# Attention with the heads' dimensions on partitions instead of tokens, in blocks of 384 tokens

## The chip, the core and the metric

The kernel runs on one core of a Trainium2 chip. TensorE (PE) multiplies matrices into PSUM, VectorE (DVE) and ScalarE (ACT) read and write PSUM and the arena in on-chip memory, and SyncE (SP) issues the DMA transfers from its queue. The metric is the device time of one execution in microseconds.

## What is computed

Linear attention over 4 batches of 576 tokens with 8 heads of 64 dimensions, a norm over each head, one dense network with 2,048 hidden units, and a mixture of 8 experts with 1,024 hidden units, whose weights come out of 8 rounds of normalizing.

```python
def _attn_ref(q, k, v, g_norm):                       # (4, 8, 576, 64)
    kv = np.einsum('bhsd,bhse->bhde', k, v)
    out = np.einsum('bhsd,bhde->bhse', q, kv)
    rms = np.sqrt(np.mean(out * out, axis=-1, keepdims=True) + 1e-06)
    return (out / rms * g_norm)

def _moe_ref(x, w_in, w_out, alpha):                  # 512 -> 2048 -> 512
    h = x @ w_in
    g = np.maximum(h, 0.0) + alpha * np.minimum(h, 0.0)
    return (g @ w_out)

def _moe2_ref(x, w_gate, w1, w2):                     # 8 experts, 512 -> 1024 -> 512
    P = normalized(np.exp(x @ w_gate - max))          # 8 rounds over rows and columns
    for e in range(E):
        out += P[:, e:e + 1] * (np.maximum(x @ w1[e], 0.0) @ w2[e])
```

The 2,304 tokens are 4 batches one behind the other, 512 features each (8 heads of 64).

## The kernel before

The large products run as 7 instead of 8 smaller ones each (a scheme of sums and differences of quarters), and each operand is split into two fp16 halves, of which three products are made. `hi_lo_mms` (line 397) issues them all: 12,240 products with 384 or 256 columns. The tokens are worked on in three pairs `p` of two blocks of 384 (`NB`); a layer `e` runs over the pairs, `Quad` units make its hidden values, `Ys` or `Outs` its results. The dense network is layers 0 and 1, the experts are layers 2 to 9. For layer 0 each pair needs the seven operands `X[m]` of x, in both halves, with features on partitions and tokens along the line.

All weights of the dense network arrive as raw words, 16 chunks for each layer, which `from_f64` turns into numbers with VectorE and ScalarE. After 8 chunks of w_in SyncE's queue holds k, v and q of the batches in an order that `FIRST` sets (line 25), then chunks of w_out. `attn_kv` (from line 435) multiplies k and v of a batch, 20 fp32 products, and writes the result into `kvbd`, 128 x 128 for two heads, with zeros between heads.

`attn_tile` makes the attention of 128 tokens, 18 times. The q tile is the stationary operand and `kvbd` streams through it (line 477), so tokens are on partitions and features along the line. ScalarE squares, VectorE sums over the 64 dimensions of each head, seven small steps on 8 columns make the inverse root with a correcting step, and VectorE multiplies by it. `attn_x` then makes the seven operands for 128 tokens of both blocks of a pair, in steps of 256 columns, into buffers of two operands, and `send` lets a DMA transpose each buffer into `X`. SyncE issues these transposes, twelve for each pair. `attn_store` copies X of pairs 0 and 1 to DRAM for layer 1. The first product that needs operand `m` waits for the transposes of it (`mx_part`).

The last two q blocks share one buffer. The first of them is loaded when the second w_in staging buffer is free (`st_free[1]`), the second when the first has been used (`load_q`).

No instruction's place is written out by hand. `Sched` is a planner: each step is a generator that yields an engine, a cost and a call, and a list scheduler with a model of each engine sets one fixed order for each engine; eight dry passes refine the due times, and the best one is issued. `T(0.87, ...)` is a TensorE step with a cost of 0.87 us. `LAGS` holds priorities. So a change to any step can move all the others. Engines then run their lists in order and wait by semaphores.

Almost every instruction of VectorE and ScalarE has line 163, where the planner issues it; on TensorE line 163 holds the small fp32 products that are issued directly.

Of the kernel before, what the change touches and what calls it, by code (L numbers as in the profile page):

```python
# [26 lines left out]
SQUARES = "000000000000000000"  # L27
# [3 lines left out]
LENT = 3  # L31
# [226 lines left out]
def fused_kernel(ctx: ExitStack, tc: tile.TileContext, qT, k, v, g_norm, w_in, w_out, alpha,  # L258
# [7 lines left out]
    nc = tc.nc  # L266
# [34 lines left out]
    def program(sc):  # L301
# [25 lines left out]
        one = const(1)  # L327
# [83 lines left out]
        x1s = [view(BR + t * 2048, F32, D) for t in range(NTILE)]  # L411
        batches = [sorted({(t * P) // S, ((t + 1) * P - 1) // S}) for t in range(NTILE)]
        kv_loaded, kv_done = [ev(2) for _ in range(4)], [ev() for _ in range(4)]
        q_loaded, q_used = [ev() for _ in range(NBLK)], [ev(TPB) for _ in range(NBLK)]
        x1_done = [ev() for _ in range(NTILE)]
# [37 lines left out]
        norm_bufs = Slots(sc, [[const(H) for _ in range(3)] for _ in range(5)])  # L453

        def by_heads(dst, x, f, **kw):
            for h in range(H):
                sl = slice(h * HD, (h + 1) * HD)
                nc.scalar.activation(dst[:, sl], x[:, sl], f, **{k_: a[:, h:h + 1] for k_, a in kw.items()})

        def attn_tile(t):  # L460

            j, o = divmod(t, TPB)
            q, x1 = qs[j], x1s[t]
            yield q_loaded[j]
            if t >= NTILE - LENT:
                yield mx_done[0]
            for b in batches[t]:
                yield kv_done[b]
            buf = yield from norm_bufs.get()
            ss, rr, tb = buf  # L470
            ps = yield from banks.get()

            def mms():
                for p in range(DC):
                    for b in batches[t]:
                        r0, r1 = max(b * S - t * P, 0), min((b + 1) * S - t * P, P)
                        nc.tensor.matmul(ps[r0:r1, p * P:(p + 1) * P], q[:, p, o * P + r0:o * P + r1],  # L477
                                         kvbd[b][:, p, :], start=True, stop=True)
            yield T(0.87 * len(batches[t]), mms)
            q_used[j].set()  # L480
            if SQUARES[t] == "1":
                yield "A", 1.93, by_heads, (x1, ps, AF.Square), dict(accum_out=ss)
            else:
                yield A(D, nc.scalar.activation, x1, ps, AF.Square)
                yield V(D, nc.vector.tensor_reduce, ss, x1.rearrange("p (h e) -> p h e", h=H), op=add, axis=AX.X)
            yield ts(H, ss, ss, 2.0 ** -20 / HD, 1e-6 * 2.0 ** -20, mult, add)
            yield A(H, nc.scalar.activation, rr, ss, AF.Sqrt)
            yield V(H, nc.vector.reciprocal, rr, rr)
            yield tt(H, tb, rr, rr, mult)
            yield tt(H, tb, tb, ss, mult)  # L490
            yield ts(H, tb, tb, -0.5, 1.5, mult, add)
            yield tt(H, rr, rr, tb, mult)
            yield [V(D, nc.vector.tensor_tensor, x1.rearrange("p (h e) -> p h e", h=H),
                     ps.rearrange("p (h e) -> p h e", h=H),
                     rr.rearrange("p (h o) -> p h o", o=1).to_broadcast([P, H, HD]), op=mult),
                   ("A", 1.93, by_heads, (x1, ps, AF.Copy), dict(scale=rr))]
            banks.put(ps)
            norm_bufs.put(buf)
            x1_done[t].set()


        MADE = (2, 0, 1, 4, 6, 5, 3)
        XPOS = [MADE.index(m_) for m_ in range(7)]
        X = view(XR, F16, 7, 2, 2 * NB).rearrange("p m a (c n) -> p m a c n", c=2)
        XF, XT = view(XR, F16, 7 * 4 * NB), view(XR, F16, 7 * 4, NB)
        half_slots = [view(TR + 18432 + i * 2048, F16, 2, D) for i in range(3)]
        lent = [view(BR + t * 2048, F16, 2, D) for t in range(NTILE - LENT, NTILE)]
        half_slots = [Slots(sc, half_slots + lent), Slots(sc, half_slots)]
        mx_split, mx_done, mx_stored = [ev(TPB) for _ in range(NP)], [ev() for _ in range(NP)], \
            [ev() for _ in range(NP)]  # L510

        def attn_x(p, o):

            even, odd = 2 * p * TPB + o, (2 * p + 1) * TPB + o
            yield x1_done[even]
            yield x1_done[odd]
            if p > 0:
                yield mx_done[0]
                yield s1_used[0][p - 1]
                yield mx_stored[p - 1]  # L520
            b11, b21, b12, b22 = [x1s[t][:, i * 256:(i + 1) * 256] for t in (even, odd) for i in range(2)]

            def send(n, buf):
                k = min(2, 7 - 2 * n)
                yield "S", 1.27, nc.sync.dma_start_transpose, (), dict(
                    out=XT[:, 8 * n:8 * n + 4 * k, o * P:(o + 1) * P], in_=buf[:, 0:k].rearrange("p k d -> p (k d)"))
                sc.dma_free = max(sc.dma_free, sc.now) + 0.45 * k
                yield sc.dma_free + 1.0
                half_slots[p > 0].put(buf)
                mx_part[p][n].set()  # L530

            bufs = []

            def put(x):
                n, k = divmod(len(bufs), 2)
# [928 lines left out]
```

## Time and profile before

| | us |
|---|---|
| median of 3 runs | 1846.12 (1844.31 to 1850.98) |
| profiled execution | 1846.93 |
| its span, first to last instruction | 1845.1 |
| TensorE busy | 1741.9 (94%), 12,808 products and as many weight loads |
| VectorE busy | 1535.5 (83%) |
| ScalarE busy | 1080.7 (59%) |
| mean granted clock of TensorE | 0.986 of 2.4 GHz |

The busy times are of the whole span. TensorE's fp32 products are recorded as two records each, so a matrix product in fp32 counts twice among the 12,808. Durations of neighbours on one engine overlap, so a mean duration is more than the distance from start to start. The page's division of the span into 40 slices shows TensorE at nine tenths or more from the sixth slice on, and at less in four of the first five, which are some 231 us.

### The profile page before, as it was taken

Reading aid. Unit: us, or ns where it says so; the run is one execution under the profiler, and the core shown is the slowest. Engines: PE = TensorE matmul, PEld = TensorE weight load, DVE = VectorE, ACT = ScalarE, POOL = GpSimd, SP = SyncE. Lnnn points to the kernel's source line nnn. Section 1 sums busy time; section 2 is a strip of 40 time slices with the busy share of each in tenths; the row PEclk is TensorE's granted clock in tenths of the full one; section 3 lists DMA queues with packets and bytes.
Section 4 is the critical chain, followed back from the end, with each engine's and each line's share of the span. In section 5 each row is a group of like instructions: output and inputs, shape, how many; then the busy total and the mean of one; then the engine's idle time right before and its main releaser. Section 6 shows DMA issues by size and latency. Waiting matters only on the chain.

```text
span 1845.1 us, 32006 instructions
## 1 busy us (share of the span) xinstructions
PE 1741.9 (94%) x12808; PEld 1251.7 (68%) x12808; DVE 1535.5 (83%) x3381; ACT 1080.7 (59%) x2290; POOL 2.5 (0%) x8
## 2 busy tenths in 40 slices
PE   4659899999999999998999999999999999999999
PEld 3435466666677766776777777677767777776777
DVE  5999696769788999699869978986998699789866
ACT  4666564535477676457646656764676556567544
POOL 0000000000000000000000000000000000000000
PEclk9789999999999999999999999999999999999999
DMA  9927411302021021112201210211122012101121
GB/s 291 256 87 189 95 62 54 121 12 86 21 106 61 12 95 47 61 47 82 76 11 47 106 61 1 81 72 61 47 83 84 1 47 106 61 1 60 59 95 35
DMA packets 70470, 137.36 MB, mean 74 GB/s; under 512 B 38960, under 2 KB 46640, under 8 KB 67632
## 3 DMA queue, kind: packets, MB, share of 16 engines
q1 hardware_dynamic: 67568, 135.28, 22.0%
q8 instruction: 100, 1.64, 0.4%
q10 hardware_dynamic: 2752, 0.03, 0.1%
q14 instruction: 50, 0.41, 0.1%
HBM read 108.55 MB, written 18.48 MB: 69 GB/s over the span
## 4 chain that ended last, share of the span: by engine, by line
PE 75%; DVE 15%; ACT 2%; DMA 2%; issue 0%; ACTq 0%; SPq 0%; DVEq 0%
PE ps L397 75%; DVE arena L163 15%; ACT arena L163 2%; DMA arena<-arena 1%; PE ps L163 0%; PE ps L683 0%; DMA arena<-in_w_in_dram 0%; ACTq L163 0%; SPq L163 0%; DVEq L163 0%
## 5 line engine op out<-in xcount | busy, mean ns | idle before, releaser
L397 PE MATMUL ps<-arena 128*128 128x256 f16 (+1 forms) x12240 | 1692.9, 301 | 72.4 <-ACT arena L163 33.9
L397 PEld LDWEIGHTS <-arena 128*128 128x128 f16 x12240 | 1200.6, 98 | 555.5 <-issue 88.3
L163 ACT ACTIVATE arena<-arena 128x384 f16<-128x384 f32 (+6 forms) x1528 | 797.1, 569 | 276.1 <-DVE arena L163 222.5
L163 DVE TENSOR_TENSOR arena<-arena 128x384 f16<-128x384 f32 (+7 forms) x1647 | 841.5, 555 | 47.5 <-ACT arena L163 43.9
L163 ACT ACTIVATE arena<-ps 128x384 f32<-128x384 f32 (+3 forms) x655 | 291.4, 451 | 410.2 <-PE ps L397 384.7
L163 DVE SCALAR_TENSOR_TENSOR arena<-ps,arena 128x384 f32<-128x384 f32 (+1 forms) x447 | 247.3, 555 | 108.9 <-PE ps L397 97.8
L163 DVE SCALAR_TENSOR_TENSOR arena<-arena 128x384 f32<-128x384 f32 (+3 forms) x526 | 283.8, 550 | 15.9 <-ACT arena L163 11.9
L163 DVE TENSOR_TENSOR arena<-ps,arena 128x256 f32<-128x256 f32 (+1 forms) x233 | 101.0, 438 | 102.5 <-ACT arena L163 73.4
L163 DVE TENSOR_REDUCE arena<-arena 128x1 f32<-128x1024 f32 (+7 forms) x148 | 112.0, 760 | 2.7 <-ACT arena L163 1.1
L163 ACT ACTIVATE arena<-ps,arena 128x384 f32<-128x384 f32 x96 | 55.1, 577 | 60.8 <-PE ps L397 57.9
L163 DVE TENSOR_SCALAR arena<-arena 128x8 f32<-128x8 f32 (+9 forms) x241 | 53.3, 235 | 5.6 <-DMA arena<-in_w_in_dram 4.8
L445 PE MATMUL ps<-arena 128*128 128x128 f32 (+1 forms) x160 | 26.2, 311 | 26.3 <-DMA arena<-in_v_dram 26.3
L445 PEld LDWEIGHTS ps<-arena 128*128 128x128 f32 (+1 forms) x160 | 22.0, 205 | 30.2 <-issue 27.1
L163 DVE TENSOR_SCALAR_CACHE_REDUCE arena<-arena 128x512 f32<-128x512 f32 x32 | 21.4, 677 | 7.5 <-ACT arena L163 7.5
L477 PE MATMUL ps<-arena 128*128 128x128 f32 (+1 forms) x160 | 18.3, 278 | 0.3 <-ACT arena L163 0.3
L477 PEld LDWEIGHTS ps<-arena 128*128 128x128 f32 (+1 forms) x160 | 17.1, 181 | 1.6 <-ACT arena L163 0.5
L163 PE MATMUL ps<-arena 128*128 128x128 f32 (+1 forms) x68 | 12.5, 265 | 0.4 <-DVE arena L163 0.4
L163 PEld LDWEIGHTS ps<-arena 128*128 128x128 f32 x68 | 11.0, 190 | 2.1 <-DVE arena L163 0.6
L163 DVE TENSOR_REDUCE arena<-ps 128x1 f32<-128x128 f32 x26 | 7.3, 284 | 5.7 <-PE ps L163 5.7
L163 ACT ACT_TABLE_LOAD x3 | 3.8, 1283 | 10.7 <-issue 10.7
L163 DVE RECIPROCAL arena<-arena 128x8 f32<-128x8 f32 (+1 forms) x34 | 7.0, 211 | 3.5 <-ACT arena L163 3.2
L163 DVE COPY arena<-ps 64x256 f32<-64x256 f32 x4 | 1.7, 414 | 5.4 <-PE ps L445 5.4
(14 smaller groups left out, 19.5 us busy)
## 6 DMA issues: line engine op xcount, KB each, us to landing
arena<-xd SPq DMA_DIRECT2D x16, 2688.0 KB, 9.4
arena<-in_w_dram SPq DMA_DIRECT2D x64, 512.0 KB, 3.7
xd<-arena SPq DMA_DIRECT2D x5, 2688.0 KB, 10.0
arena<-in_w_in_dram SPq DMA_DIRECT2D x16, 512.0 KB, 4.8
arena<-in_w_out_dram SPq DMA_DIRECT2D x16, 512.0 KB, 4.8
arena<-in_qT_dram SPq DMA_DIRECT2D x6, 768.0 KB, 11.7
out_dram<-arena SPq DMA_DIRECT2D x36, 128.0 KB, 1.7
arena<-in_k_dram SPq DMA_DIRECT2D x4, 1024.0 KB, 9.4
```

The costliest lines, as they stand in the source:

```text
L163: way[2](*way[3], **way[4])
L397: r = nc.tensor.matmul(ps[:, 0:ncols], x, y, start=(start and i == 0 and m == 0), stop=(stop and i == n - 1 and m == 2), skip_group_check= ...
L445: nc.tensor.matmul(ps[:, sl], kt[0:n, c, sl], vt[0:n, c, sl], start=(c == 0), stop=(c == 4))
L477: nc.tensor.matmul(ps[r0:r1, p * P:(p + 1) * P], q[:, p, o * P + r0:o * P + r1], kvbd[b][:, p, :], start=True, stop=True)
```

## The change

The product is turned round: `kvbd` is stationary and a block of 384 tokens of q streams through it, so the result has features on partitions, as `X` wants it. `attn_block(j)` handles 384 tokens, six times. `attn_part` makes 128 features of it (two heads): one fp32 product with 384 columns, on ScalarE the square and a copy out of PSUM, and the sum of squares as three products of the square with `heads`, a constant of two columns that has ones for one head each. All sums of a block are then 24 columns with tokens on partitions. The small steps are as before, on 24 columns. To multiply by it, three products with the identity turn it to 8 partitions (`turn_mms`), ScalarE copies it, and `spread` multiplies by a constant that spreads each head's value over its 64 partitions (384 columns), after which VectorE multiplies. `attn_x` makes the operands straight into X in steps of 384 columns. Transposes, their buffers (`half_slots`, `lent`) and `send` are gone, and units wait for each operand (`mx_made`) instead. Two of the 28 buffers between the layers' halves hold the spreading constant first and wait for `spread_done`; the fourth buffer of units opens when all squares and spreads are used.

```diff
-        def attn_tile(t):
...
+        def attn_block(j):
...
+            sums = yield from banks.get()
+            squared = ev(DC)
+            for c in range(DC):
+                sc.add(attn_part(j, c, sums, squared), sc.task.first_lag - 0.1)
+            yield squared
             buf = yield from norm_bufs.get()
             ss, rr, tb = buf
+            n = TPB * H
+            yield ts(n, ss, sums[:, 0:n], 2.0 ** -20 / HD, 1e-6 * 2.0 ** -20, mult, add)
...
+            def turn_mms():
+                for o in range(TPB):
+                    nc.tensor.matmul(ps[0:H, o * P:(o + 1) * P], rr[:, o * H:(o + 1) * H], ident, start=True, stop=True)
+            yield T(0.45, turn_mms)
+            rt = yield from sq_bufs.get()
+            yield A(NB, nc.scalar.activation, rt[0:H], ps[0:H, 0:NB], AF.Copy)
...
+            def spread(c):
+                ps = yield from banks.get()
+                yield T(0.4, nc.tensor.matmul, ps[:, 0:NB], spreads[0:H, c, :], rt[0:H], start=True, stop=True)
+                yield tt(NB, x1[:, c, :], x1[:, c, :], ps[:, 0:NB], mult)
...
+        def attn_part(j, c, sums, squared):
+            ps = yield from banks.get()
+
+            def mms():
+                for b in batches[j]:
+                    r0, r1 = max(b * S - j * NB, 0), min((b + 1) * S - j * NB, NB)
+                    nc.tensor.matmul(ps[:, r0:r1], kvbd[b][:, c, :], qs[j][:, c, r0:r1], start=True, stop=True)
+            yield T(0.4, mms)
+            q_used[j].set()
+            sq = yield from sq_bufs.get()
+            yield A(NB, nc.scalar.activation, sq, ps[:, 0:NB], AF.Square)
+            yield A(NB, nc.scalar.activation, ys[j][:, c, :], ps[:, 0:NB], AF.Copy)
+            banks.put(ps)
+
+            def sum_mms():
+                for o in range(TPB):
+                    nc.tensor.matmul(sums[:, o * H + 2 * c:o * H + 2 * c + 2], sq[:, o * P:(o + 1) * P], heads,
+                                     start=True, stop=True)
+            yield T(0.45, sum_mms)
...
-            def send(n, buf):
-                k = min(2, 7 - 2 * n)
-                yield "S", 1.27, nc.sync.dma_start_transpose, (), dict(
...
+            def put(m_, x):
+                yield from halves(X[:, XPOS[m_], 0, c, :], X[:, XPOS[m_], 1, c, :], x)
+                mx_made[p][m_].set()
...
```

The order moves at the start of TensorE's list. Before, products of tiles (line 477) stand between those of k and v (line 445), and behind the fourth of these the first fp16 products of layer 0 follow (line 397), with the tiles of the last blocks among them:

```order
16 L477 MATMUL ps_67<-arena 128x128 x4
17 L477 MATMUL ps_65<-arena 128x128 x4
18 L445 MATMUL ps_69<-arena 128x128 x20
19 L397 LDWEIGHTS arena
20 L397 MATMUL ps_64<-arena 128x384
```

After, the same place of TensorE's list (k and v at line 443, products of parts at 513, sums at 523, turns at 485, spreads at 161, layer 0 at 395):

```order
29 L443 MATMUL ps_65<-arena 128x128 x20
30 L485 MATMUL ps_64<-arena 8x128 x3
31 L523 MATMUL ps_68<-arena 128x2 x6
...
45 L513 MATMUL ps_70<-arena 128x192 x2
46 L523 MATMUL ps_67<-arena 128x2 x12
47 L513 MATMUL ps_64<-arena 128x384
48 L513 MATMUL ps_71<-arena 128x384
49 L513 MATMUL ps_65<-arena 128x384
50 L513 MATMUL ps_70<-arena 128x384
51 L523 MATMUL ps_66<-arena 128x2 x12
52 L395 LDWEIGHTS arena
53 L395 MATMUL ps_64<-arena 128x384
```

Here row 45 ends the products of the block before the last, which two batches share (192 columns each), and rows 47 to 50 are those of the last block. All blocks' products and sums, and the spreads of the first two blocks, now stand ahead of the first product of layer 0; the spreads of the other four stand among layer 0's products.

SyncE's queue before, from the first chunks of w_out on:

```order
21 L163 DMA arena<-in_w_out_dram 128x1024 x3
22 L163 DMA_TRANSPOSE arena<-arena 128x8x128 x8
23 L163 DMA_TRANSPOSE arena<-arena 128x4x128
24 L163 DMA_TRANSPOSE arena<-arena 128x8x128
25 L163 DMA_TRANSPOSE arena<-arena 128x4x128 x2
26 L163 DMA arena<-in_w_out_dram 128x1024
27 L163 DMA xd<-arena 128x10752
28 L163 DMA arena<-in_qT_dram 128x4x384
29 L163 DMA arena<-in_w_out_dram 128x1024 x3
30 L163 DMA arena<-in_qT_dram 128x4x384
```

And after:

```order
21 L161 DMA arena<-in_w_out_dram 128x1024 x3
22 L161 DMA arena<-in_qT_dram 128x4x384
23 L161 DMA arena<-in_w_out_dram 128x1024
24 L161 DMA arena<-in_qT_dram 128x4x384
25 L161 DMA arena<-in_w_out_dram 128x1024 x2
26 L161 DMA xd<-arena 128x10752
```

The twelve transposes of the first pair are gone from between the chunks and the last two q blocks, and those blocks' loads move up.

## Rows read from the trace of the kernel before

**Rows 1.** Busy us (records) by stretch: PE, PEld, DVE, ACT, POOL; clock, DMA share, GB/s.

```profile
26.33:63.99 37.66, 37.31 (x262) 32.60 (x262) 27.46 (x100) 22.17 (x45) 0.00 (x0) 1.00 1.11 319
63.99:117.90 53.91, 35.51 (x204) 21.17 (x204) 52.07 (x157) 31.70 (x70) 0.00 (x0) 0.81 0.57 173
117.90:135.72 17.82, 0.36 (x4) 0.10 (x1) 17.82 (x53) 12.46 (x30) 0.00 (x0) 0.65 0.21 60
135.72:182.80 47.08, 45.72 (x264) 26.41 (x264) 43.64 (x103) 31.41 (x69) 0.00 (x0) 0.95 0.68 180
182.80:220.40 37.60, 28.58 (x165) 16.66 (x165) 26.39 (x65) 17.51 (x42) 0.00 (x0) 0.91 0.39 68
220.40:330.30 109.90, 109.90 (x677) 66.31 (x677) 84.33 (x180) 63.87 (x120) 0.00 (x0) 1.00 0.22 78
```

**Rows 2.** TensorE in order of time: start, length, records [idle before, what ended it].

```profile
26.33 8.19 PE L445 MATMUL ps<-arena 128*128 128x128 f32 x40 [26.33 <-DMA arena<-in_v_dram]
...
37.39 5.98 PE L445 MATMUL ps<-arena 128*128 128x128 f32 x40
43.31 2.05 PE L477 MATMUL ps<-arena 128*128 128x128 f32 x16
...
53.44 4.73 PE L477 MATMUL ps<-arena 128*128 128x128 f32 x40
58.01 5.98 PE L445 MATMUL ps<-arena 128*128 128x128 f32 x40
67.73 1.36 PE L397 MATMUL ps<-arena 128*128 128x384 f16 x6 [3.73 <-DMA arena<-arena]
72.72 2.10 PE L397 MATMUL ps<-arena 128*128 128x384 f16 x6 [3.64 <-DMA arena<-arena]
...
218.40 0.38 PE L163 MATMUL ps<-arena 128*128 128x128 f32 x2
218.62 1.14 PE L397 MATMUL ps<-arena 128*128 128x384 f16 x6
220.40 64.02 PE L397 MATMUL ps<-arena 128*128 128x384 f16 x393 [0.64 <-DVE arena L163]
```

**Rows 3.** SyncE's queue in order of time: start, length, transfers issued.

```profile
46.89 1.96 SPq L163 DMA_DIRECT2D arena<-in_w_out_dram  x3
56.02 23.75 SPq L163 DMA_TRANSPOSE arena<-arena  x12
...
81.79 0.38 SPq L163 DMA_DIRECT2D arena<-in_qT_dram  x1
...
101.17 0.38 SPq L163 DMA_DIRECT2D arena<-in_qT_dram  x1
```

**Rows 4.** Groups by shape up to 200 us: count, busy us, mean ns, idle before.

```profile
L163 DVE TENSOR_TENSOR arena<-arena 128x256 f16<-128x256 f32 x42 | 16.5, 419 | 3.7 <-ACT arena L163 3.5
L163 DVE TENSOR_TENSOR arena<-arena 128x384 f16<-128x384 f32 x29 | 15.5, 552 | 0.9 <-ACT arena L163 0.9
L163 DVE TENSOR_REDUCE arena<-arena 128x8 f32<-128x512 f32 x18 | 12.0, 677 | 1.2 <-ACT arena L163 1.1
L163 DVE TENSOR_TENSOR arena<-ps,arena 128x512 f32<-128x512 f32 x17 | 11.5, 684 | 0.0
L163 DVE TENSOR_TENSOR arena<-arena 128x8 f32<-128x8 f32 x54 | 7.7, 158 | 0.0
L163 ACT ACTIVATE arena<-ps 128x384 f32<-128x384 f32 x4 | 1.8, 477 | 0.0
```

**Rows 5.** TensorE in order of time, from 601.95 us: an fp32 pair of 8 columns.

```profile
601.95 0.28 PE L163 MATMUL ps<-arena 128*128 128x8 f32 x2
602.09 3.09 PE L397 MATMUL ps<-arena 128*128 128x384 f16 x18
```

**Rows 6.** DMA issues from 80 to 120 us: size, median us to landing.

```profile
arena<-in_qT_dram SPq DMA_DIRECT2D x2, 768.0 KB, 7.9
```

**Rows 7.** The chain that ended last, to 250 us: start, length, what.

```profile
135.72 8.21 PE ps L397 x36
```

More of the change, by code (lines that the diff above doesn't have):

```diff
@@ L30 @@
 MIX = 0.4
-LENT = 3
 MARGIN = 0.8
@@ L451, in attn_kv @@
             kv_done[b].set()
[L453 to L458, printed above, removed]
-        def attn_tile(t):
-            j, o = divmod(t, TPB)
-            q, x1 = qs[j], x1s[t]
+        norm_bufs = Slots(sc, [[const(TPB * H) for _ in range(3)] for _ in range(2)])
@@ new lines, in spread @@
+            def spread(c):
+                ps = yield from banks.get()
+                yield T(0.4, nc.tensor.matmul, ps[:, 0:NB], spreads[0:H, c, :], rt[0:H], start=True, stop=True)
+                yield tt(NB, x1[:, c, :], x1[:, c, :], ps[:, 0:NB], mult)
+                banks.put(ps)
+                x1_done[j][c].set()
+                done.set()
+            for c in (0, 2, 1, 3):
+                sc.add(spread(c), sc.task.first_lag)
+            yield done
+            sq_bufs.put(rt)
@@ L471, in attn_tile @@
+            sq_used.set()
+            spread_done.set()
+        def attn_part(j, c, sums, squared):
             ps = yield from banks.get()
             def mms():
[L474 to L478, printed above, removed]
@@ L488, in attn_tile @@
[L488 to L496, printed above, removed]
@@ L512, in attn_x @@
[L512 to L516, printed above, removed]
+        XF = view(XR, F16, 7 * 4 * NB)
+        mx_split, mx_stored = [ev(2) for _ in range(NP)], [ev() for _ in range(NP)]
+        mx_made = [[ev(2) for _ in range(7)] for _ in range(NP)]
+        def attn_x(p, c):
+            for j in range(2 * p, 2 * p + 2):
+                yield x1_done[j][c]
+                yield x1_done[j][2 + c]
             if p > 0:
-                yield mx_done[0]
@@ L552, in attn_x @@
+            yield from put(0, b11)
+            yield tt(NB, b11, b12, b11, sub)
+            yield from put(4, b11)
+            yield tt(NB, b12, b22, b12, sub)
+            yield tt(NB, b11, b22, b11, sub)
+            yield from put(5, b11)
+            yield from put(6, b12)
+            yield from put(1, b21)
+            yield tt(NB, b21, b21, b11, sub)
+            yield from put(2, b22)
+            yield from put(3, b21)
             mx_split[p].set()
-        mx_part = [[ev(TPB) for _ in range(4)] for _ in range(NP)]
@@ L1368, in program @@
             nc.gpsimd.memset(one, 1.0)
+            nc.gpsimd.memset(heads, 0.0)
+            for i in range(2):
+                nc.gpsimd.memset(heads[i * HD:(i + 1) * HD, i:i + 1], 1.0)
             nc.gpsimd.memset(view(W2R + 8192, F32, 4 * D), 0.0)
         def gains():
+            yield 10.0
+            yield V(D, nc.vector.tensor_copy, spreads[0:H].rearrange("p c (h e) -> p (c h) e", h=2),
+                    ident[0:H, 0:H].rearrange("p (h o) -> p h o", o=1).to_broadcast([H, H, HD]))
+            spread_ready.set()
             yield 10.5
```

92 lines of the change are left out of this document (33 added, 59 removed).

## The prediction

> **What bounds the kernel now.** I read the busy times by stretch first, then TensorE's own instructions in order of time, then the DMA queue. From 220.40 us TensorE is busy for all of its stretch at full clock [rows 1], and 393 fp16 products follow each other in 64.02 us, 163 ns each [rows 2]; the slices of the page behind it look the same. So TensorE is the limit from about 220 us on, and the change touches nothing there. The place to look is what stands before. TensorE starts at 26.33 us, when the first v has landed [rows 2]. By 220.40 some 564 of the 12,240 fp16 products of line 397 are done (the counts of rows 1 less the fp32 records): 91.9 us at 163 ns. The fp32 products (lines 445 and 477, and the maxima at 163) are 37.3 us in the stretch from 26.33 to 63.99 [rows 1], and some 7.3 us behind it, 44.6 us in all. The rest, 220.4 - 26.3 - 91.9 - 44.6 = **57.6 us, is TensorE waiting or running at the low clock**. That is what the change can win from.
>
> Three stretches hold it. From 63.99 to 117.90 TensorE is busy for 35.5 of 53.9 us at a mean clock of 0.81, and VectorE for 52.1; from 117.90 to 135.72 TensorE does almost nothing and VectorE is busy for all 17.82; from 182.80 to 220.40 TensorE lacks another 9 us [rows 1]. So VectorE is the limit over most of it. The first cause is ahead of that: layer 0's first products start at 67.73 and 72.72, each after a wait for a DMA inside the arena, a transpose [rows 2]. SyncE's queue holds 12 transposes one behind the other from 56.02 for 23.75 us, and the loads of the last two q blocks stand behind them, at 81.79 and 101.17 [rows 3].
>
> **The change, part by part.** *Transposes.* All 36 go, with the waits for them. The q loads then stand right behind the third chunk of w_out, issued by 49 us [rows 3].
>
> *VectorE.* Removed, by durations: a reduction and a product of 512 columns per tile, 18 x (677 + 684 ns) = 24.5 us; 109 small ones at 158 ns, 17.2 us; 99 steps of the split at 419 ns, 41.5 us; 83 us in all [rows 4]. Added: 24 products and 66 steps of the split with 384 columns, at 552 ns, 49.7 us, and 36 small ones, 5.7 us; 55 us. That is 28 us less by durations (less than that in time, since neighbours overlap a little). *ScalarE* gets 54 passes from PSUM at 477 ns, 26 us [rows 4], for 18 longer ones; it has room, busy for 22.2 of 37.7 us up to 63.99 [rows 1].
>
> *TensorE pays.* A 128-column fp32 product is two records, and 40 records of line 477 take 58.01 - 53.44 = 4.57 us: 0.228 us a product [rows 2]. What is added has no row of its own. The 24 wide products (384 columns) at three narrow ones each, 0.68 us, are 16.4 us, for the 17.1 us of line 477 that go. The 24 spreads (384 columns, 8 rows) are 16.4 us again, and more where 8 rows stand between 128: line 445, where each fifth product has 64 rows, takes 43.31 - 37.39 = 5.92 us for its 40 records [rows 2], 0.34 us more for each such change, and the order has some 11 groups: 3.7 us. The 72 sums have two columns, but each loads 128 x 128 fp32 weights twice; the nearest row is a pair of records with 8 columns between fp16 products, 0.14 us from its start to the next one's [rows 5]. That is the lower end, 10.1 us; since here load follows load, I take the 0.228 of line 477, 16.4 us. The 18 turns are 4.1 us. In sum 57.0 - 17.1 = **40 us more on TensorE**, all of it before 220 us. With wide products and spreads at fp16's price of 163 ns a record, 0.33 us, and the lower end for the sums it is 17 us.
>
> The wide price decides. If the 114 ns of line 477 are the load of its weights and not the stream of its columns, the lower end holds. Against it: the two fp32 records of 128 columns that start at 218.40 keep the fp16 product behind them waiting until 218.62 [rows 2], 110 ns each, as if their stream took that long; so I take the upper end. The Trainium skill (FP8 and Floating Point Precision, TensorE Precision Notes) says that true FP32 takes four passes through the array; by that a wide product is some 0.64 us, an estimate, and the sum 2 us less. The Trainium skill (TensorE: Matmul & The Clock Gate, LDWEIGHTS) makes a load's time hang on its columns alone, which speaks for the lower end; no run here shows a wide fp32 product.
>
> *Where it lies.* The order puts all six blocks' products and sums, and two blocks' spreads, ahead of the first fp16 product. TensorE has then 26 us of line 445, 1.5 us of maxima, 16.4 of wide products, 16.4 of sums, 1.4 of turns and 7 of spreads to do, 69 us from 26.3: the first fp16 product comes near **95 us plus waits**, against 67.73. Before, 204 records of any kind follow up to 117.90 [rows 1], so most of this delay is in a time that was poorly used.
>
> *New waits.* The last q block shares its buffer with the one before and is loaded only when TensorE has used that; a q block lands after 7.9 us (the median of the two last ones) [rows 6], of which 12 sums cover 2.7: 5 us on TensorE, with all of layer 0 behind it. The last block's squares cost one more. After a pause TensorE comes back at the low clock: 36 products took 8.21 us from 135.72 [rows 7] instead of 5.9: 2.3 us. Behind that TensorE and VectorE go side by side. From 135.72 to 182.80 VectorE was busy for 43.6 and TensorE for 45.7 of 47.1 us [rows 1], a loss of 3%; 3 us over the next 100. Together **11.5 us** of the 57.6 come back. Nothing else hides behind TensorE's longer start: what VectorE saves is worth little while TensorE is late itself.
>
> *Sum.* 57.6 - 40 - 11.5 = 6 us won. The profiled execution took 1846.9 us (span 1845.1), the median of the runs is 1846.1; 1846.9 - 6 = **1841 us**.
>
> **Rivals.** *TensorE's additions are cheap.* With the lower ends 23 us less stand on TensorE, its first fp16 product comes near 75 us, and VectorE is the limit again, with up to 28 us less to do: a gain of some 22, 1825 us. For it: 114 ns may be the load. Against: the wait at 218.40.
>
> *Nothing is won.* The waits are not 11.5 but 18 to 24 us: the products of layer 0 also stand behind the spreads of four more blocks, each after a chain of small steps on VectorE. 1847 to 1853 us.
>
> *Slower, through VectorE's fixed order.* The planner prices a wide product at 0.4 us and three sums at 0.45, less than the rows give, so it places VectorE's steps ahead of results that come later. While TensorE works off the attention, VectorE then stands still, as it did from 26.33 to 63.99, busy for 27.5 of 37.7 us [rows 1], only until 95 us now. Some 110 us of its work are left for the 120 us of TensorE that follow. If VectorE falls behind once more as it did from 117.90 to 135.72, another 17.8 us of waiting come to the 11.5: 29 us, and 1858 us. It decides from 18 us of waits on.
>
> *The start hangs on something else*, so that the change does not do what it says: the loads run at 319 GB/s up to 63.99 [rows 1], the same before and after. But TensorE's own work is longer than the loads, so this has no chance of its own.
>
> **How the numbers follow.** Forecast, 1841, its own range 1833 to 1847: 0.48. Cheap additions: 0.20. Nothing won: 0.20. Slower: 0.12. About 0.5% (9 us) is what a measurement of this kernel can tell from no change. Faster by more is under 1836.9: the cheap case and two fifths of the forecast, 0.40. Slower by more is over 1855.3: the last case, 0.12. Between lie 0.48. The range, 1822 to 1855, leaves out a third of the cheap case and most of the slow one. The plan is made anew for the whole kernel, so what follows 220 us can shift by a few us either way.
>
> **What would show it.** Right: no transposes; the first fp16 product between 92 and 102 us; 40 us more of fp32 on TensorE; the 564th fp16 product near 214 us, and no gap from there. A wide record of about 330 ns says that the price is right, one of 163 that the first rival is. A pause on TensorE of 3 to 6 us ahead of the last q block is the new wait. Wrong: the first fp16 product before 85 us; VectorE busy at over 95% between 95 and 200 us with TensorE waiting for it (the slow rival); or a difference that arises after 250 us, which nothing here foresees.

## The result, and the profile after

The changed kernel takes 1871.83 us, the median of four runs (1863.75 to 1875.24), beside 1847.32 us for the kernel before on the same chip: a ratio of 1.0125, 95% interval 1.0088 to 1.0163. It is slower by 24.5 us; 1841 was forecast, with a range up to 1855. The execution that was profiled took 1872.41 us.

Counting TensorE's fp16 products in order of start tells where. The first one starts at 110.7 us (before: 67.7), the 564th at 233.8 (219.4), the 800th at 274.4 (258.6). From the 800th to the 6000th the distance stays between 15.1 and 18.2 us; then it grows to 25.2 at the last. So there are two losses: **some 16 us up to 250 us, and another 9 us behind 1000 us**.

These stretches of the changed kernel answer to [rows 1]. The columns are the same: length, busy us with records of TensorE, its weight loads, VectorE, ScalarE, GpSimd, then the granted clock, the DMA share and GB/s. The first ends with the first fp16 product, the second with the last spread; the last line lies inside the first two.

```profile
26.25:110.67 84.42, 84.07 (x402) 67.55 (x403) 41.86 (x107) 45.61 (x96) 0.00 (x0) 0.82 0.51 169
110.67:160.41 49.74, 46.65 (x186) 23.01 (x186) 34.62 (x92) 22.21 (x46) 0.00 (x0) 0.77 0.23 88
160.41:233.80 73.39, 73.39 (x439) 43.58 (x439) 69.61 (x145) 52.33 (x105) 0.00 (x0) 0.97 0.27 95
233.80:330.00 96.20, 94.67 (x582) 56.95 (x581) 83.00 (x180) 59.38 (x113) 0.00 (x0) 1.00 0.17 56
...
26.00:180.00 154.00, 150.31 (x693) 101.76 (x694) 92.85 (x228) 79.54 (x164) 0.00 (x0) 0.81 0.38 128
86.00:107.00 21.00, 21.00 (x74) 18.13 (x75) 12.29 (x23) 11.20 (x26) 0.00 (x0) 0.52 0.28 88
```

Look at the first number of TensorE and at the clock together. Before, TensorE idled: 35.51 of 53.91 us busy, then 0.36 of 17.82 [rows 1]. Now it is busy for 150.31 of 154 us, and VectorE, which was saturated there, for only 92.85. The waits are gone, and yet TensorE is later. The clock says why: it is 0.81 over these 154 us, and from 86 to 107 us it is 0.52 while TensorE is busy for **21.00 of 21.00 us**. In the kernel before the low clock stood beside TensorE's waits. At 0.81, 0.19 x 154 = 29 us of full-speed work are lost.

TensorE in order of time (start, length, records, idle before), the lines that answer to [rows 2]:

```profile
26.25 10.24 PE L443 MATMUL ps<-arena 128*128 128x128 f32 x40 [26.25 <-DMA arena<-in_v_dram]
...
46.07 2.84 PE L523 MATMUL ps<-arena 128*128 128x2 f32 x24
...
98.49 5.12 PE L523 MATMUL ps<-arena 128*128 128x2 f32 x24
103.47 4.66 PE L513 MATMUL ps<-arena 128*128 128x384 f32 x8
107.97 2.84 PE L523 MATMUL ps<-arena 128*128 128x2 f32 x24
110.67 4.72 PE L395 MATMUL ps<-arena 128*128 128x384 f16 x18
117.91 11.34 PE L395 MATMUL ps<-arena 128*128 128x384 f16 x60 [2.52 <-ACT arena L161]
...
132.84 2.20 PE L161 MATMUL ps<-arena 8*128 8x384 f32 x6
134.97 1.15 PE L395 MATMUL ps<-arena 128*128 128x384 f16 x6
...
154.99 5.48 PE L161 MATMUL ps<-arena 8*128 8x384 f32 x8 [0.57 <-ACT arena L161]
160.41 74.67 PE L395 MATMUL ps<-arena 128*128 128x384 f16 x444
```

Line 523 is the sums, 513 the wide products, 485 the turns, and the 8x384 products of line 161 are the spreads. Twelve sums, 24 records, take 2.84 us at 46.07 and 5.12 at 98.49: the same work at either level of the clock. Eight records of spreads take 5.48 us at 154.99. From 160.41 on TensorE runs for 74.67 us without a gap.

One loss at the very start is not in these clocks. The first 40 records of line 443 take 10.24 us and the next 40 like them 5.98, yet the views print a clock of 1.00 there. The kernel before has the same 40 records and took 8.19 us for them; over all traces of this study they take 7.7 to 10.95 us, whatever the edit. So the place of a product in one execution can differ by up to 3 us for no reason of its edit.

In SyncE's queue the transposes of [rows 3] are gone. The last two q blocks are issued at

```profile
77.09 0.38 SPq L161 DMA_DIRECT2D arena<-in_qT_dram  x1
...
98.73 0.38 SPq L161 DMA_DIRECT2D arena<-in_qT_dram  x1
```

hardly earlier than before (81.79 and 101.17); the last one waits for TensorE's own products now.

### The profile page after: what moved, and what is told of

The parts are those of the page before. It is cut to its first block, busy times and chain, and to the rows that moved or that the text cites. A ratio compares the mean times of both kernels' runs of the same rounds, so it can differ in the third digit from the quotient of the medians.

```text
span 1870.5 us, 32040 instructions
## 1 busy us (share of the span) xinstructions
PE 1807.0 (97%) x12940; PEld 1293.1 (69%) x12940; DVE 1522.7 (81%) x3263; ACT 1091.9 (58%) x2288; POOL 2.8 (0%) x11
## 4 chain that ended last, share of the span: by engine, by line
PE 72%; DVE 14%; ACT 2%; DMA 1%; issue 0%; SPq 0%; DVEq 0%
PE ps L395 71%; DVE arena L161 14%; ACT arena L161 2%; DMA arena<-in_w_out_dram 0%; PE ps L161 0%; PE ps L691 0%; DMA arena<-in_w_in_dram 0%; SPq L161 0%; DVEq L161 0%
## 5 line engine op out<-in xcount | busy, mean ns | idle before, releaser
L395 PE MATMUL ps<-arena 128*128 128x384 f16 (+1 forms) x12240 | 1699.0, 302 | 31.8 <-DVE arena L161 18.7
L161 ACT ACTIVATE arena<-arena 128x384 f16<-128x384 f32 (+3 forms) x1498 | 795.0, 577 | 240.1 <-DVE arena L161 190.4
L161 DVE TENSOR_TENSOR arena<-arena 128x384 f16<-128x384 f32 (+6 forms) x1578 | 836.3, 574 | 50.4 <-ACT arena L161 46.8
L161 DVE TENSOR_TENSOR arena<-ps,arena 128x256 f32<-128x256 f32 x216 | 90.0, 420 | 101.2 <-ACT arena L161 77.6
L161 DVE TENSOR_REDUCE arena<-arena 128x1 f32<-128x1024 f32 (+5 forms) x130 | 99.7, 772 | 0.6
L443 PE MATMUL ps<-arena 128*128 128x128 f32 (+1 forms) x160 | 29.8, 340 | 26.3 <-DMA arena<-in_v_dram 26.3
L161 DVE TENSOR_SCALAR arena<-arena 128x1 f32<-128x1 f32 (+9 forms) x208 | 48.0, 244 | 5.8 <-DMA arena<-in_w_in_dram 4.8
L443 PEld LDWEIGHTS ps<-arena 128*128 128x128 f32 (+1 forms) x160 | 25.2, 231 | 31.2 <-issue 28.6
L161 PE MATMUL ps<-arena 128*128 128x128 f32 (+2 forms) x116 | 35.5, 410 | 1.2 <-DVE arena L161 0.7
L513 PE MATMUL ps<-arena 128*128 128x384 f32 (+1 forms) x64 | 25.0, 554 | 0.3 <-ACT arena L161 0.3
L523 PEld LDWEIGHTS ps<-arena 128*128 128x128 f32 x144 | 22.2, 237 | 3.2 <-issue 1.3
L513 PEld LDWEIGHTS ps<-arena 128*128 128x128 f32 x64 | 16.3, 275 | 5.6 <-issue 3.6
```

The source lines that it names most:

```text
L161: way[2](*way[3], **way[4])
L395: r = nc.tensor.matmul(ps[:, 0:ncols], x, y, start=(start and i == 0 and m == 0), stop=(stop and i == n - 1 and m == 2), skip_group_check= ...
L443: nc.tensor.matmul(ps[:, sl], kt[0:n, c, sl], vt[0:n, c, sl], start=(c == 0), stop=(c == 4))
L513: nc.tensor.matmul(ps[:, r0:r1], kvbd[b][:, c, :], qs[j][:, c, r0:r1], start=True, stop=True)
L523: nc.tensor.matmul(sums[:, o * H + 2 * c:o * H + 2 * c + 2], sq[:, o * P:(o + 1) * P], heads, start=True, stop=True)
```

## The experiments

Two theories stood against each other. **The clock**: the small fp32 products (sums of 2 columns, spreads of 8 rows) let the granted clock fall to half although TensorE never stops. **The order**: the slow rival of the prediction; the planner's prices are too low, VectorE's steps stand in a wrong order, and TensorE pays for it in another way. A third question is the 9 us behind 1000 us. The table has all runs. The ratios are to the kernel before on the same chip (several chips were used, and its median was 1847.3 to 1849.5 us on them); the clock is that of 26 to 180 us; the last columns give the start of the 800th fp16 product and the time from there to the last one. These three are of the one execution that was profiled, which for e3_spread128 and e8_spread64 was 5.8 and 3.9 us shorter than the median. A label is explained at its run.

| kernel | median us | ratio, 95% interval | clock | 800th at | 800th to last |
|---|---|---|---|---|---|
| before | 1847.32 | | 0.88 | 258.6 | 1582.6 |
| changed | 1871.83 | 1.0125 [1.0088, 1.0163] | 0.81 | 274.4 | 1592.0 |
| e1_prices | 1872.23 | 1.0134 [1.0119, 1.0149] | 0.81 | 269.6 | 1596.2 |
| e2_sums40 | 1865.36 | 1.0095 [1.0077, 1.0113] | 0.88 | 265.1 | 1591.7 |
| e3_spread128 | 1850.56 | 1.0017 [1.0004, 1.0029] | 0.94 | 250.3 | 1588.5 |
| e4_both | 1847.05 | 0.9997 [0.9988, 1.0006] | 0.98 | 249.7 | 1590.9 |
| e8_spread64 | 1857.03 | 1.0049 [1.0031, 1.0067] | 0.93 | 255.2 | 1591.9 |
| e6_prices_both | 1846.99 | 0.9996 [0.9981, 1.0010] | 0.98 | 248.9 | 1595.5 |
| e7_lags_both | 1830.27 | 0.9903 [0.9875, 0.9930] | 1.00 | 237.8 | 1586.4 |
| e9_prices_lags | 1863.51 | 1.0070 [1.0041, 1.0100] | 0.81 | 270.8 | 1583.7 |
| e11_lags_shapes | 1848.45 | 1.0001 [0.9988, 1.0014] | 0.97 | 252.4 | 1587.4 |
| e12_no_sums40 | 1836.48 | 0.9929 [0.9910, 0.9947] | 0.93 | 246.9 | 1584.8 |
| e5_before_replan | 1849.83 | 1.0010 [0.9995, 1.0024] | 0.88 | 256.4 | 1585.4 |
| e10_before_lags | 1851.76 | 1.0016 [1.0003, 1.0028] | 0.89 | 251.0 | 1592.7 |

### Real prices alone (e1_prices)

```diff
-            yield T(0.45, turn_mms)
+            yield T(0.67, turn_mms)
...
-                yield T(0.4, nc.tensor.matmul, ps[:, 0:NB], spreads[0:H, c, :], rt[0:H], start=True, stop=True)
+                yield T(0.68, nc.tensor.matmul, ps[:, 0:NB], spreads[0:H, c, :], rt[0:H], start=True, stop=True)
...
-            yield T(0.4, mms)
+            yield T(0.68, mms)
...
-            yield T(0.45, sum_mms)
+            yield T(0.69, sum_mms)
```

> Only the planner's prices change: 0.68 us for a product and a spread of 384 columns instead of 0.4, 0.69 for three sums and 0.67 for three turns instead of 0.45, as the trace has them. If the time was lost because VectorE's steps were placed ahead of results that come later (the slow rival of the prediction), the order mends itself and 10 to 17 us come back, near 1857. If it was lost in the attention through a granted clock of half while TensorE is busy, the same instructions meet the same clock: within 5 us of the changed kernel, and the granted clock of 86 to 107 us stays near 0.55. The plan of all layers is made anew, so the stretches of low clock at the layers' ends, after 1000 us, may come or go either way, 3.4 us of low clock costing 1.7.

Measured: 1872.23 us, as the changed kernel, with the same clock of 0.81, and 0.58 from 86 to 107 us. The planner's prices alone don't hold the time. It isn't quite without effect: the 800th product comes 4.8 us earlier, and the new plan gives 4.2 of them back behind it.

### Sums with more columns (e2_sums40)

```diff
-                    nc.tensor.matmul(sums[:, o * H + 2 * c:o * H + 2 * c + 2], sq[:, o * P:(o + 1) * P], heads,
-                                     start=True, stop=True)
+                    i = o * DC + c
+                    nc.tensor.matmul(sums[:, i * 40:(i + 1) * 40], sq[:, o * P:(o + 1) * P],
+                                     heads.rearrange("p (g t) -> p g t", g=1).to_broadcast([P, 20, 2]),
+                                     start=True, stop=True)
...
-            yield ts(n, ss, sums[:, 0:n], 2.0 ** -20 / HD, 1e-6 * 2.0 ** -20, mult, add)
+            yield ts(n, ss.rearrange("p (i t) -> p i t", t=2), sums[:, 0:480].rearrange("p (i t) -> p i t", t=40)[:, :, 0:2], 2.0 ** -20 / HD, 1e-6 * 2.0 ** -20, mult, add)
```

> Each of the 72 sums streams 40 columns (the two, repeated 20 times) instead of 2; two of the 40 are read. Order and plan are the same. At 40 columns two records stream less long than a load of 128 weight columns takes, so at full clock a record should keep its 0.118 us. If the few columns are what lets the granted clock fall while TensorE is busy, the clock from 86 to 107 us rises from about 0.55 to over 0.8, the sums' 5.12 us for 24 records goes back to 2.84, and the kernel is 6 to 12 us faster. If the clock hangs on something else, it stays at 0.5 and the time within 3 us. If a stream can't lie under the load, 72 x 2 x 17 ns, 2.4 us, are added.

Measured: 6.5 us less than the changed kernel, the 800th product 9.3 us earlier. TensorE in order of time shows that 20 times the columns cost 1% while the clock is full, and that the late group of 12 sums is back from 5.12 us; the stretch 86 to 107 us now has

```profile
42.99 2.87 PE L524 MATMUL ps<-arena 128*128 128x40 f32 x24
...
91.45 2.77 PE L524 MATMUL ps<-arena 128*128 128x40 f32 x24
96.07 2.85 PE L513 MATMUL ps<-arena 128*128 128x384 f32 x8 [1.85 <-DMA arena<-in_qT_dram]
```

and a clock of 0.89. The idle 1.85 us is the wait for the last q block, the new wait of the prediction. In the changed kernel TensorE was too late itself to meet it.

### Spreads with 128 rows (e3_spread128), and both (e4_both)

```diff
-                yield T(0.4, nc.tensor.matmul, ps[:, 0:NB], spreads[0:H, c, :], rt[0:H], start=True, stop=True)
+                yield T(0.4, nc.tensor.matmul, ps[:, 0:NB], spreads[:, c, :], rt, start=True, stop=True)
...
             nc.gpsimd.memset(heads, 0.0)
+            nc.gpsimd.memset(view(HR + 40960, F32, 4 * P), 0.0)
+            nc.gpsimd.memset(view(TR + 18432, F32, 4 * NB), 0.0)
```

> The 24 spreads use 128 rows, 120 of them with zero weights, instead of 8; order and plan are the same. Two things are told apart: the price of going from 8 rows to 128 and back, and the clock. If the 8 rows are what lets the clock fall, the stretches from 137 to 149 and from 155 to 167 us run at over 0.85 instead of 0.5 to 0.65: some 8 us less. If only the change of rows costs, 2 to 4 us less (11 changes at 0.34). If neither, within 2 us.

> Both edits of the two runs before, sums with 40 columns and spreads with 128 rows. If the shape of the small fp32 products sets the clock, the low stretches of the start (some 58 us of records at half clock while TensorE is busy) are mostly gone and 15 to 22 us come back, near 1852; the first fp16 product comes near 98 us instead of 110.7. If the clock falls for another reason, within 4 us of the changed kernel. The 9 us lost at the layers' ends stay in any case.

Measured: 1850.56 and 1847.05 us, both beyond what was expected. The spreads alone give back 21.3 us of the loss, not some 8: beside the last eight records of spreads, which went from 5.48 to 2.85 us, the sums gained too, though they are as before. Their late group of 12 takes 2.74 us for 5.12. Why the clock held there is not shown. TensorE in order of time in e3_spread128:

```profile
86.77 2.74 PE L523 MATMUL ps<-arena 128*128 128x2 f32 x24
...
135.70 2.85 PE L161 MATMUL ps<-arena 128*128 128x384 f32 x8 [0.57 <-ACT arena L161]
```

With both, all of the loss in the start is gone: the 800th product comes at 249.7 us, 24.7 earlier, and 8.9 earlier than in the kernel before. The clock of 26 to 180 us went from 0.81 to 0.94 and 0.98: 0.17 x 154 = 26 us. (From 137 to 149 us, where the changed kernel has 0.57, both runs read 1.00, but they are nearly through with their spreads by then, so that stretch compares other work.) The stretch of e4_both in which some low clock is left, busy times as above:

```profile
86.00:107.00 21.00, 15.52 (x84) 10.57 (x84) 19.40 (x49) 17.63 (x40) 0.00 (x0) 0.87 0.54 202
```

Order, plan, counts and data of all other products are the same in these three runs and in the changed kernel: TensorE's 12,940 records follow in the same order in all four traces. So the shape of the small products set the clock. What is left at 0.87 lies beside waits again: TensorE is busy for 15.52 of 21 us, VectorE for 19.40.

### How many rows (e8_spread64)

```diff
-                yield T(0.4, nc.tensor.matmul, ps[:, 0:NB], spreads[0:H, c, :], rt[0:H], start=True, stop=True)
+                yield T(0.4, nc.tensor.matmul, ps[:, 0:NB], spreads[0:64, c, :], rt[0:64], start=True, stop=True)
```

(with the two memsets of the run before)

> The spreads use 64 rows, 56 of them with zero weights; order and plan as in the changed kernel. With 8 rows the kernel takes 1872, with 128 rows 1850.6. If each change of the row count costs the 0.34 us that line 445 shows for 64 rows, and the clock follows the rows in use, it comes between: 1855 to 1868, with some 25 to 45 us at half clock in the start (58 with 8 rows, 17 with 128). If any use of fewer rows than 128 is what costs, it stays near 1872; if 8 rows alone are too few, near 1851.

Measured: 1857.03 us, the clock 0.93, the 800th product 4.9 us after that of 128 rows and 19.2 before that of 8. This separates the clock from the price of a change of rows, which is the same for 64 rows as for 8. That price stands in TensorE's order of time: three spreads of 128 rows between fp16 products at full clock, in e3_spread128, then three of 64 rows between wide products, in e8_spread64:

```profile
119.45 2.10 PE L161 MATMUL ps<-arena 128*128 128x384 f32 x6
121.39 1.14 PE L395 MATMUL ps<-arena 128*128 128x384 f16 x6
```

```profile
79.72 2.20 PE L161 MATMUL ps<-arena 64*128 64x384 f32 x6
81.85 0.91 PE L513 MATMUL ps<-arena 128*128 128x384 f32 x2
```

From start to start it is 1.94 us with 128 rows, 81.85 - 79.72 = 2.13 with 64, and 134.97 - 132.84 = 2.13 us with 8 rows in the changed kernel. A group of spreads thus pays 0.19 us for its two changes of rows; 11 groups are 2 us of the 24.7.

### The order, once the clock is mended (e6_prices_both, e7_lags_both)

Both have the edits of e4_both and the prices of e1_prices; the second also

```diff
-LAGS = {"in": -1.7, "out": -1.4, "attn1": -1.2, "attn2": -1.1, "x0": -1.5, "x1": -0.8, "x2": -0.8, "w1": -1.6, "w2": -1.3,
+LAGS = {"in": -1.7, "out": -1.4, "attn1": -1.6, "attn2": -1.1, "x0": -1.5, "x1": -0.8, "x2": -0.8, "w1": -1.6, "w2": -1.3,
```

> Sums with 40 columns, spreads with 128 rows, and the planner's prices as the trace has them (0.68, 0.69, 0.67). With the clock mended, does VectorE's order matter? With the prices alone, 800 products were reached 4.8 us earlier, but the total was the same. If the order costs something of its own, 800 products come 3 to 6 us earlier than in the kernel with both shapes alone (249.7 us); if not, within 2 us. The total carries the new plan's layers' ends: 1838 to 1855 us.

> As the run with both shapes and the real prices, and blocks 2 and 3 of the attention get more precedence (lag -1.6 instead of -1.2), a plan made anew. A try at a version faster than both kernels: low-clock time in the start as in the kernel with both shapes (6.8 us), so 800 products near 246 to 251 us against 258.6 before, and the total near 1838 if the idle time at the layers' ends lies apart, near 1850 if it lies close together as in the changed kernel.

Measured: the prices by themselves bring the 800th product 0.8 us forward. (The first 40 records took 1.8 us longer in this execution, so the plan itself may be worth 2.6.) This run has the plan of e1_prices with other shapes, and so is a second pair for the shapes, in another order: the 800th product comes 20.7 us earlier and the time is 25.2 us less. With the lag the 800th product comes at 237.8 us, 20.8 before that of the kernel before and earlier than expected, and the kernel takes 1830.27 us: **the fastest of all, 0.9903 of before (0.9875 to 0.9930) and 41.6 us below the changed one**. Its attention, from the first product to the first fp16 product, and five lines of TensorE in order of time:

```profile
26.16:98.80 72.64, 72.00 (x424) 57.34 (x425) 53.92 (x141) 51.67 (x110) 0.00 (x0) 1.00 0.66 218
```

```profile
26.16 8.05 PE L443 MATMUL ps<-arena 128*128 128x128 f32 x40 [26.16 <-DMA arena<-in_v_dram]
34.14 0.71 PE L161 MATMUL ps<-arena 128*128 128x128 f32 x4
35.20 2.85 PE L513 MATMUL ps<-arena 128*128 128x384 f32 x8 [0.35 <-ACT arena L161]
37.88 5.98 PE L443 MATMUL ps<-arena 128*128 128x128 f32 x40
...
92.26 2.20 PE L513 MATMUL ps<-arena 128*128 128x384 f32 x6 [0.30 <-DMA arena<-in_qT_dram]
```

### Which of the three edits does it (e9_prices_lags, e11_lags_shapes, e12_no_sums40)

Each takes one edit out of the fastest version: both shapes, the real prices, or the 40 columns of the sums alone (the diffs above, undone).

> The fastest version so far (1830) without its shapes: sums of 2 columns and spreads of 8 rows as in the changed kernel, the real prices, and -1.6 for the lag of blocks 2 and 3. The order is that of the fastest version. If the shapes work through the clock, half-clock stretches of 30 to 58 us come back in the start (none in the fastest version), 800 products are reached at 252 to 268 us instead of 237.8, and the time is 1845 to 1860. If the better order keeps the clock up by itself, within 5 us of 1830.

> The fastest version without the real prices: the changed kernel with both shapes and the lag of -1.6. If the prices did nothing, it is near 1830 with 800 products near 238 us; if they keep VectorE's steps where their operands are ready, 800 products come 3 to 10 us later and the time is 1834 to 1845.

> The fastest version with its sums back at 2 columns; spreads of 128 rows, real prices and the lag of -1.6 stay, and so does the order. In the changed kernel's order the sums' 40 columns gave 9.3 us by 800 products while the spreads had 8 rows, and only 0.6 us once those had 128. If the two shapes stand in for each other, 800 products come at 237 to 242 us and the time is 1830 to 1836. If the sums alone still lower the clock, as after the groups of 24 in the changed kernel, 5 to 15 us come back.

Measured: without the shapes 1863.51 us, 33.2 more, in the very same order, and more than was expected (1860 at most). This is the cleanest pair of the study, the third order in which the shapes decide. The stretch that took 72.64 us at clock 1.00 takes 98.17, with TensorE as busy as there:

```profile
26.80:124.97 98.17, 97.83 (x424) 72.07 (x425) 57.50 (x146) 54.34 (x113) 0.00 (x0) 0.77 0.52 170
```

0.77 x 98.17 = 75.6 us at full speed; 22.6 of the 25.5 us that were added are the clock. Of the rest 2.1 us are the start, where the same 40 records took 10.19 us for 8.05, and 8 groups of spreads at 0.19 us are some 1.5. Ten executions of e9_prices_lags spread from 1850.34 us at a mean clock of 0.987 to 1872.56 at 0.977: the same program, and 0.010 x 1850 = 18.5 of these 22.2 us are again the clock. The longest execution of the fastest version took 1834.80.

Without the real prices the kernel takes 1848.45 us and the 800th product comes 14.6 us later, more than the 3 to 10 expected. So the order has a part after all, with TensorE no longer slowed down. That the right prices do it, and not the chance of another plan, is not shown: it is one plan against one, and in the order of e4_both the same prices gave 0.8 us. TensorE in order of time (e11_lags_shapes) has waits that the fastest version doesn't have:

```profile
106.76 1.14 PE L395 MATMUL ps<-arena 128*128 128x384 f16 x6 [4.22 <-ACT arena L161]
108.98 1.45 PE L485 MATMUL ps<-arena 128*8 128x128 f32 x6 [1.08 <-DVE arena L161]
...
147.49 0.50 PE L395 MATMUL ps<-arena 128*128 128x384 f16 x2 [1.38 <-ACT arena L161]
```

With these and two shorter ones some 8 us are waits, and the low clock around them, 0.97, accounts for 0.03 x 154 = 5.

With 2 columns in the sums it is 1836.48 us and a clock of 0.93. The sums matter by 9.1 us here, against 0.6 in the order of e4_both, where TensorE then waited for others instead: from 26 to 180 us it was idle for 6.8 us in e4_both, for 4.1 in e3_spread128.

### The loss behind 1000 us (e5_before_replan, e10_before_lags)

All idle time of TensorE from 250 to 1820 us is 26.2 us in the kernel before and 28.1 in the changed one, hardly more (the 25.1 and 27.6 in the expectation below are a little low). Around the layers' ends the clock differs. Busy times around 1200 us, of the kernel before and of the changed one:

```profile
1192.00:1204.00 12.00, 8.64 (x73) 6.88 (x71) 12.00 (x25) 7.06 (x16) 0.00 (x0) 1.00 0.59 229
```

```profile
1215.00:1227.00 12.00, 8.85 (x62) 6.58 (x60) 12.00 (x25) 6.43 (x14) 0.00 (x0) 0.86 0.60 229
```

TensorE is busy for about the same time, and the clock is 0.86 instead of 1.00, 1.7 us lost. The changed kernel has five such stretches behind 600 us, 23.9 us at half clock together, the kernel before one of 6.8: (23.9 - 6.8) / 2 = 8.5 of the 9.4 us. The change touches no code there, but the planner makes a new plan for the whole kernel. Two controls give the kernel before a new plan, by a price of 0.91 instead of 0.87 for a tile's products, and by the lag of -1.6:

> The kernel before with one number changed: the planner's price of a tile's four fp32 products is 0.91 us instead of 0.87 (by the trace 4 x 0.228). The work is the same, only the plan is made anew. The changed kernel loses 9 us behind 1000 us, where its idle time is nearly that of before (27.6 us against 25.1 behind 250 us) but lies closer together, with 23.9 us at half clock behind 600 us against 6.8. If that is a chance of the plan and not of the change, this kernel moves by several us too, to either side, and its low-clock time at the layers' ends differs from 6.8 us. If the time stays within 2 us of before, with as little low clock, the changed kernel's loss there belongs to the change.

> The kernel before with the lag of tiles 6 to 11 at -1.6 instead of -1.2, nothing else. A control for the fastest version: if precedence for these blocks helps any kernel, this one is faster than 1840; if it helps only where the products of layer 0 are not behind transposes, within 6 us of before. It is also a third plan of the kernel before: from 800 products to the last the two seen took 1582.6 and 1585.4 us, with 6.8 us at half clock each, the changed kernel's plans 1586 to 1596. If the loss at the layers' ends is a chance of the plan, this one lies anywhere from 1580 to 1596.

Measured: the first left the time nearly as it was (2.2 us more), with 1585.4 us from the 800th product on and as little low clock. By what was expected of it that spoke for the change as the cause. The second overturned this: 1592.7 us, as much as the changed kernel's 1592.0, with 17.1 us at half clock behind 600 us and the same dips in code without the change:

```profile
1190.00:1202.00 12.00, 8.14 (x56) 6.24 (x56) 12.00 (x24) 5.59 (x12) 0.00 (x0) 0.86 0.59 229
1363.00:1375.00 12.00, 9.11 (x71) 7.26 (x69) 11.58 (x23) 5.73 (x13) 0.00 (x0) 0.86 0.47 201
```

Three plans of the kernel before lie between 1582.6 and 1592.7, those with the change between 1583.7 and 1596.2. They overlap: a new plan alone can bring a loss of this size, and one plan with the change (e9_prices_lags, e12_no_sums40) has hardly any of it. So it belongs to the plan that a kernel happens to get. Even one plan varies, by 3.5 us: the changed kernel, e2, e3, e4 and e8 share theirs. The controls also show that the start of the kernel before had room: with the lag it reached the 800th product 7.6 us earlier, and lost that at the layers' ends.

## Why the prediction was wrong

**What bounds the kernel** was read rightly: TensorE from about 220 us, and 57.6 us of waits and low clock before. The changed kernel did remove the waits there: from 26 to 160 us 0.35 + 2.52 + 0.57 = 3.4 us are left.

**The prices** held. A wide product is 2.68 / 4 = 0.67 us (37.88 - 35.20 in the fastest version; 0.68 was taken from the upper end), twelve sums 48.77 - 46.07 = 2.70 us, 0.225 each (0.228). The lower end, fp16's price, is out. The Trainium skill (FP8 and Floating Point Precision, TensorE Precision Notes) has true FP32 pass through the array four times; at that rate a wide product is an estimated 0.64 us, and the trace agrees within 5%. Only the changes of rows were over-priced, 0.34 against 0.19 us for a group. At full clock the whole of the new fp32 work is what was forecast: from start to start an estimated 24 x 0.67 + 72 x 0.225 + 24 x 0.65 + 18 x 0.25 = 52.4 us (spreads 1.94 / 3; three turns take 0.75 in e3_spread128), where the prediction had 57.0 with 3.7 for changes of rows, 53.3 without. Its groups in the fastest version, count, busy us and mean ns:

```profile
L161 PE MATMUL ps<-arena 128*128 128x384 f32 x48 | 17.9, 492 | 0.0
L524 PE MATMUL ps<-arena 128*128 128x40 f32 x144 | 17.3, 278 | 0.0
L513 PE MATMUL ps<-arena 128*128 128x384 f32 x32 | 12.1, 502 | 0.6 <-ACT arena L161 0.3 <-DMA arena<-in_qT_dram 0.3
...
L513 PE MATMUL ps<-arena 128*128 128x192 f32 x32 | 6.1, 335 | 0.0
L485 PE MATMUL ps<-arena 128*8 128x128 f32 x36 | 4.9, 273 | 0.0
```

In sum 58.3 us of busy time, in which neighbours overlap. The same groups of the changed kernel add up to 75.7:

```profile
L161 PE MATMUL ps<-arena 8*128 8x384 f32 x48 | 23.1, 616 | 0.6 <-ACT arena L161 0.6
...
L523 PE MATMUL ps<-arena 128*128 128x2 f32 x144 | 22.0, 282 | 0.0
L513 PE MATMUL ps<-arena 128*128 128x384 f32 x32 | 14.7, 602 | 0.3 <-ACT arena L161 0.3
L513 PE MATMUL ps<-arena 128*128 128x192 f32 x32 | 10.3, 505 | 0.0
...
L485 PE MATMUL ps<-arena 128*8 128x128 f32 x36 | 5.6, 296 | 0.0
```

**The step that failed** is the sum of these durations in "Where it lies", the 40 us more on TensorE. It multiplied counts by durations that came from stretches at full clock, and so took for granted that a TensorE which never stops keeps that clock. Low clock came into the sum only after a pause, as 2.3 us. It was 29 us, 58 us at half clock, and of the eight falls of the clock up to 160 us only two stand at a pause of TensorE (2.52 and 0.57 us). "Near 95 us plus waits" for the first fp16 product shows it: 110.67 us were measured, and 0.18 x 84.42 = 15 us of that is the clock, which leaves 95.5.

The Trainium skill (TensorE: Matmul & The Clock Gate, Part 1) ties the clock to how busy TensorE is and tells to avoid its idle gaps. By that, if the records' busy time is what counts as busy, this stretch should have run at full clock; the trace differs, 0.52 over 21.00 us that were busy throughout. The prediction had no rival of this kind, and its bounds didn't hold it.

**The new waits**, 11.5 us, were over-sized and partly of another kind. The wait for the last q block (5 us) does not appear in the changed kernel, where TensorE came to it late, at 103.47, without a gap: the sums ahead of it took 5.12 us for the 2.7 of the forecast, and the block landed 4.5 us after it was issued, not 7.9. In e2_sums40, with the sums back at 2.77, the wait is 1.85 us. The loss beside VectorE (3 us) did not come at all: from 160.41 to 233.80 TensorE is busy for 73.39 of 73.39 us. In one line: 252.6 us were forecast for the 800th product (258.6 - 6); 29 us of clock instead of 2.3, and 3.4 us of waits instead of 9.2, make 273.5. Measured were 274.4. That it comes so near is in part luck: the 2 us more at the start (10.24 for 8.19) and the 1.7 us less for the changes of rows (11 x 0.15) are not in it.

**The rivals.** The slow one named the right sign, 1858 us, and a wrong cause: its sign in the profile, VectorE busy at over 95% between 95 and 200 us with TensorE waiting, is not there: from 110.67 to 160.41 us VectorE was busy for 34.62 of 49.74 us, and from there to 233.80 for 69.61 of 73.39, where TensorE never waited. Waits of its kind appear in the order of e11_lags_shapes, once TensorE was fast, as part of 14.6 us; that the prices caused them is not shown. *Cheap additions* fell with the price. *Nothing is won* had the waits too large, 18 to 24 us for 3.4.

**Behind 250 us** the prediction allowed the new plan "a few us either way" and named a difference there as something that nothing foresaw. It was 9.4 us, and the plans seen spread over 14.

**What the change could do** was under-rated: with the clock kept up and the planner given the true prices and one other lag, the same change takes the kernel to 1830.27 us. That is near the rival that had assumed cheap products (1825), but by another way: the products cost what the forecast said.

## What to carry to other kernels

Before a price from one stretch is used in another, look at the granted clock of both: a TensorE that is busy all the time isn't always at full clock, and products with few rows or few columns are where to look. Filling such products up (zero rows, repeated columns) cost at most 1% of their own time here and gave back 25 to 33 us in three orders. And where a planner orders the whole kernel, time it also with plans that the edit doesn't need: here plans of the same code differed by 10 us far from any edit.

## What the runs showed of the hardware

The granted clock went from 2.4 to 1.2 GHz while TensorE was busy for 21.00 of 21.00 us, in the midst of fp32 products of 2 columns and of 8 rows; with 40 columns and 128 rows, in one and the same order, it stayed at 2.4 for the attention behind the first 40 records (1.00 against 0.77). Either shape alone left part of the loss: 0.88 with the columns only, 0.94 with the rows only, 0.98 with both, 0.81 with neither, in the order of the changed kernel. The rows that were added held zero weights, and most of the columns were not read. Whether other values in them would do the same wasn't tried, nor what exactly the chip looks at. With 64 rows the clock was 0.93 against 0.94 with 128 and 0.81 with 8.

An fp32 product with 128 rows and 40 columns takes 1% more than one with 2 (24 records, 2.87 us and 2.84): its columns are not what it takes its time for here. And three products with 8 rows between ones with 128 take 0.19 us more than three with 128 rows.
